# The last pair's second layer directly behind its first, and w_out by product in DRAM, in a decayed linear attention with a softplus feed-forward layer

## The chip, the cores and the metric

One core of one Trainium2 chip runs the whole program. The metric is device time in microseconds (us). The kernel before took 552.56 us in the median of three runs (551.27, 552.56 and 556.31).

## What is computed

The reference, cut to what matters: a linear attention with per-head decay over blocks of 64 positions, 4 sequences of 768 positions with 8 heads of 64, and on its output x (3072 tokens by 512) two layers with a softplus between them.

```python
for b in range(nb):                                   # 12 blocks of 64
    intra = einsum('bhic,bhjc->bhij', qb, kb) * Dmask
    intra = einsum('bhij,bhjd->bhid', intra, vb)
    inter = einsum('bhid,bhde->bhie', qb * lam_pow, kv_state)
    out[:, :, sl] = intra + inter
    kv_state = lam_block * kv_state + einsum('bhsd,bhse->bhde', kb * rev_pow, vb)
h = x @ w_in                                          # 3072x512 @ 512x2048
g = maximum(h, 0) + log1p(exp(-abs(h)))
y = g @ w_out                                         # 3072x2048 @ 2048x512
```

## The kernel before, in words

The program makes x in six chunks of 512 columns (c = 0 to 5), each from four head pairs; a unit g is one chunk of one head pair. Each chunk goes through the two layers in three pairs of chunks, (0,1), (2,3) and (4,5), which the code names 0, 2 and 4. Every float32 operand of the layers is split into a rounded part and a rest (`hi` on ScalarE, `lo` on VectorE), and each product is three TensorE matmuls (`m`, `n`: three per quarter in chunk pair 0; `product` and `out_product`: three per piece).

For pairs 2 and 4 the first layer, and for all pairs the second, multiplies blocks of two by two with seven products instead of eight, P1 to P7, as Strassen's method does in the form with few sums. The sums of weight blocks that it needs are made on VectorE (`in_sums`, `second_sums`), split, and kept in DRAM: `g1`, `g2` for w_in, `v_sums` (four sums per block i) and `g3` (the plain w_out, by block i) for w_out. `load_w1` reads back both parts for a block i of the first layer. `load_v(c, p, m)` reads what product p of the second layer needs for four blocks, one half m: for P5, P6, P7 and P3 one DMA of 1 MB from `v_sums`, for P1, P2 and P4 four DMAs of 256 KB from `g3`.

The softplus outputs of a pair are eight tiles `act` of 1 MB, one per block i, each with four quarters. Pairs 0 and 2 write them to DRAM (`put_by`, steps `wr` and `wrm`) and read them back by quarter (`fetch`, step `rd`, into tiles `back`); pair 4's stay in SBUF until used.

On-chip tiles come from fixed places. The tables `homes` give each new tile its place (21 of 8 KB per partition, `b8`, and smaller kinds), so a tile that takes a place waits for the last reader of the tile before it, also where that reader is a DMA that stores it.

The order of all work but the last two second layers is a written list of some 1500 steps, each a word and its numbers, which one loop turns into instructions; an engine runs its own in that order. Words that matter here: `L` loads weights or a unit; `xy`, `z`, `x`, `y` are attention on TensorE; `pr`/`px` are the first layer's products of pairs 2 and 4 and `cu2`, `cu3`, `c1` the ScalarE copies of a product out of PSUM, `u2b`, `c11` and so on VectorE sums; `s11` to `s22` softplus, `t3` a VectorE difference; `sumB`, `plB`, `sndB` make, split and send block i of `v_sums`; `w1`, `w1c` are `load_w1`; `lvb`, `thb`, `tlb`, `ob` are load, `hi`, `lo` and products of the second layer in the list. In the kernel before that is pair 0, from tiles `back`, mixed with the end of pair 4's first layer. Behind the list a loop does the second layers of pairs 4 and 2, one product after another; at the start of each it loads the weights of the next, and `fetch_at` says when pair 2's outputs are read back. The last matmuls are cut into two halves of 256 columns, so that the sum and the store of the first half overlap the second half.

All loads and nearly all stores are issued by one queue, SP's, in the list's order.

Of the kernel before, what the change touches and what calls it, by code (L numbers as in the profile page):

```python
# [32 lines left out]
def decay_attention_softplus_ffn(  # L33
# [236 lines left out]
    def w_hi(*ks):  # L270
        nc.scalar.copy(out=w_at(ks)[:, 0], in_=c_at(ks).bitcast(F32))

    def w_lo(*ks):
        w = w_at(ks)
        nc.vector.tensor_sub(out=w[:, 1], in0=c_at(ks).bitcast(F32), in1=w[:, 0])

    def w_of(f, which):
        j, i = divmod(w_order.index((f, which)), 2)
# [531 lines left out]
    for c, word in ((0, "b"), (2, ""), (4, "c")):  # L810
# [11 lines left out]
        "thb": lambda p, i: split_hi(0, p, i), "tlb": lambda p, i: split_lo(0, p, i),
        "thc": lambda i: split_hi(4, "P1", i), "tlc": lambda i: split_lo(4, "P1", i), "lvc": lambda m: load_v(4, "P1", m),
        "lvb": lambda p, m: load_v(0, p, m),
        "ob": lambda p, i: [out_product(0, p, i, n) for n in range(2)],
        "tkb": lambda p, n: taking(0, p, n),
        "sdb": lambda p, n: send(*taken[0, p, n], n, nc.sync),
# [6 lines left out]
    for line in """  # L834
        scan 3, scan 1, scan 0, scan 2, mk64, Lq 3, x 3, a 3, Lq 0, lpm, L A0, scale A0, shift A0, lps, x 0, Lv 3, z 3,
        xh 3, Lq 1, a 0, xl 3, round A0, Lk 0, Lv 0, Lk 3, x 1, k 0, sign A0, add A0, Lq 2, L A2, a 1, L A3, Lv 2,
        L u4, Lk 1, Lk 2, Lv 1, k 3, z 0, xh 0, rp1, y 0, xl 0, lamc, y 3, st 0, x 2, hi A0, lo A0, st 3, scale A2 A3,
        m 0 0, a 2, z 2, round A2 A3, shift A2 A3, sign A2 A3, xh 2, xl 2, add A2 A3, m 0 2, k 4, xy 4, q 4, L A1, a 4,
        k 1, m 0 3, k 2, uh 4, hi A2 A3, lo A2 A3, y 1, st 1, z 4, xh 4, xl 4, round A1, y 2, scale A1, m 2 3, m 2 0,
        shift A1, ul 4, m 2 2, st 2, L u5, k 5, m 3 0, z 1, xh 1, xy 5, q 5, sign A1, add A1, hi A1, L u8, k 8, q 8,  # L840
        n 0 0, xl 1, m 0 1, m 2 1, uh 5, a 5, ul 5, L u7, q 7, lo A1, z 5, L A4, xy 8, act 0, xh 5, act 2, xl 5, a 8,
        m 1 2, m 3 1, uh 8, ul 8, L A5, kv 8, scale A4 A5, m 3 3, shift A4 A5, n 2 0, k 7, sign A4 A5, m 1 3,
        round A4 A5, add A4 A5, z 8, xr 8, L B0, xy 7, hi A4 A5, m 1 1, uh 7, a 7, ul 7, m 1 0, act 1, n 2 1, lo A4 A5,
        sum 1, n 0 1, n 1 0, L u6, k 6, q 6, m 3 2, act 3, z 7, xh 7, xl 7, xy 6, uh 6, L B1, L u9, m 4 0, sum 2,
        m 4 2, m 4 1, kv 9, n 0 3, a 6, L A8, scale B0 B1, m 4 3, q 9, L A9, act 4, n 2 3, ul 6, z 6, k 9, xh 6, xl 6,
        ph 1, pl 1, L u10, xy 9, L A7, m 5 0, a 9, kv 10, L u12, k 10, L A6, n 2 2, bct 2, uh 9, m 5 3, ul 9, n 1 2,
        scale A8 A9, shift A8 A9, sign A8 A9, scale A6 A7, n 1 1, shift A6 A7, n 0 2, n 1 3, bct 1, n 3 3, z 9, bct 0,
        L A11, xy 10, a 10, sA 0, n 5 3, L u11, sign A6 A7, xr 9, round A6 A7, add A6 A7, k 11, round B0 B1,
        round A8 A9, L u13, uh 10, ul 10, L A10, ph 2, n 4 3, n 5 2, scale A10 A11, n 3 2, n 5 0, q 10, add A8 A9,
        pl 2, n 4 2, n 5 1, shift B0 B1, n 4 0, bct 5, n 4 1, L A13, hi A6 A7, L A12, z 10, t3b 0, bct 4, sA 1, xr 10,  # L850
        xy 11, m 5 2, kv 11, kv 12, n 3 0, n 3 1, bct 3, lo A6 A7, snd 1, L A14, n 7 3, n 6 0, m 5 1, k 12, n 6 3,
        shift A10 A11, q 11, snd 2, uh 11, ul 11, sign A10 A11, round A12 A13, a 11, act 5, round A10 A11, add A10 A11,
        n 6 2, n 7 0, xy 12, z 11, hi A10 A11, m 6 3, a 12, uh 12, ul 12, m 6 2, sum 5, m 7 2, L A15, m 7 3,
# [186 lines left out]
```

## Time and profile before

| what | value |
|---|---|
| median of three runs | 552.56 us |
| profiled execution, its own time | 560.41 us |
| its span, first to last instruction | 558.6 us |
| TensorE busy | 540.0 us, 97% of the span |
| VectorE, ScalarE busy | 423.4 us, 311.5 us |
| moved by DMA | 180.08 MB, mean 322 GB/s |
| mean granted TensorE clock | 0.997 |

The profile is of one execution, and that one took 7.85 us more than the median of the runs. "Idle before" in a row is the time that an engine stood still just before the group's instructions, with what ended it. Matmuls overlap in the record: one of 512 columns lasts some 390 ns from start to end, but the next starts sooner, so the pace is busy time by count. A TensorE clock of 1.00 is 2.4 GHz, 0.50 is 1.2 GHz.

### The profile page before, as it was taken

The numbers are of one execution on the slowest core, as the hardware profiler recorded it, in microseconds if no ns is written. First come the engines' busy times: TensorE is split into PE (matmuls) and PEld (weight loads), VectorE is DVE, ScalarE is ACT, GpSimd is POOL, SyncE is SP. The second block draws the span as 40 slices with busy tenths as digits, with TensorE's granted clock in tenths as the row PEclk, the third lists the DMA queues.
The fourth block names the chain that finished last, engine by engine and source line by source line (L and its number), as shares of the span: only waits on it lengthen the run. The fifth ranks groups of instructions, "written<-read, shape, count | busy, mean of one in ns | idle before, by whom it ended". The sixth has DMA issues, their size and how long they took to land.

```text
span 558.6 us, 11757 instructions
## 1 busy us (share of the span) xinstructions
PE 540.0 (97%) x4777; PEld 441.9 (79%) x4777; DVE 423.4 (76%) x681; ACT 311.5 (56%) x520; POOL 0.4 (0%) x5
## 2 busy tenths in 40 slices
PE   8989998999999997999998999998999999999997
PEld 6668887888888886888886778887878888888886
DVE  6898899899966768797743588686795796865982
ACT  4855875666755467677533636654554445455440
POOL 0000000000000000000000000000000000000000
PEclk9999999999999999999998999999999999999999
DMA  8998999999999999999999999968298799983751
GB/s 304 402 407 341 322 346 381 350 408 373 337 394 381 375 380 364 402 325 397 378 368 336 283 345 371 366 217 266 86 318 311 237 385 342 374 318 94 246 191 74
DMA packets 76424, 180.08 MB, mean 322 GB/s; under 512 B 5074, under 2 KB 25810, under 8 KB 71762
## 3 DMA queue, kind: packets, MB, share of 16 engines
q1 hardware_dynamic: 75648, 178.15, 88.1%
q10 hardware_dynamic: 722, 1.18, 0.6%
q8 instruction: 38, 0.62, 0.4%
q14 instruction: 16, 0.13, 0.1%
HBM read 124.78 MB, written 54.53 MB: 321 GB/s over the span
## 4 chain that ended last, share of the span: by engine, by line
PE 74%; DMA 16%; DVE 4%; ACT 2%; issue 2%; SPq 1%; ACTq 0%; DVEq 0%
PE h L460 16%; PE r2P L709 14%; PE r4P L709 12%; PE r0P L709 11%; PE x L585 9%; PE c L585 4%; DMA att<-in_att 3%; DMA v_sums<-box 3%; PE x L364 2%; DMA v0P<-v_sums 2%; DMA g<-w 2%; PE a L585 2%; DMA back<-kept 2%; PE z L378 2%; PE z L382 2%
## 5 line engine op out<-in xcount | busy, mean ns | idle before, releaser
L460 PE MATMUL h<-x,w 128*128 128x512 f32 x384 | 93.5, 397 | 2.5 <-issue 1.4
L460 PEld LDWEIGHTS h<-x,w 128*128 128x128 f32 x384 | 70.6, 188 | 19.4 <-issue 2.3
L709 PE MATMUL r0P<-s0P,v0P 128*128 128x512 f32 x336 | 77.5, 390 | 2.7 <-DMA v0P<-v_sums 2.5
L709 PE MATMUL r2P<-s2P,v2P 128*128 128x512 f32 (+1 forms) x348 | 76.7, 382 | 0.5 <-DVE post L991 0.5
L709 PE MATMUL r4P<-s4P,v4P 128*128 128x512 f32 x336 | 76.6, 390 | 0.3 <-DMA v4P<-v_sums 0.3
L709 PEld LDWEIGHTS r0P<-s0P,v0P 128*128 128x128 f32 x336 | 62.8, 188 | 16.9 <-ACT s0P L675 3.2
L709 PEld LDWEIGHTS r2P<-s2P,v2P 128*128 128x128 f32 x348 | 63.9, 188 | 13.4 <-DVE post L991 0.7
L709 PEld LDWEIGHTS r4P<-s4P,v4P 128*128 128x128 f32 x336 | 63.0, 188 | 13.7 <-ACT s4P L675 0.7
L675 ACT CAST s0P<-back 128x512 fp32r<-128x512 f32 x40 | 24.0, 620 | 31.5 <-PE r0P L709 11.3
L675 ACT CAST s2P<-back 128x512 fp32r<-128x512 f32 x40 | 24.3, 622 | 23.8 <-PE r2P L709 9.8
L675 ACT CAST s4P<-act 128x512 fp32r<-128x512 f32 x40 | 24.7, 622 | 21.8 <-PE r4P L709 10.2
L680 DVE TENSOR_TENSOR s4P<-act,s4P 128x512 fp32r<-128x512 f32 x40 | 26.8, 688 | 13.0 <-ACT s4P L675 12.9
L680 DVE TENSOR_TENSOR s2P<-back,s2P 128x512 fp32r<-128x512 f32 x40 | 26.5, 687 | 12.1 <-ACT s2P L675 12.1
L777 ACT COPY ta<-x 128x512 f32<-128x512 f32 x32 | 18.4, 586 | 30.1 <-PE x L585 30.1
L763 ACT ACTIVATE act<-act 128x512 f32<-128x512 f32 x48 | 29.7, 631 | 6.6 <-DVE act L766 5.7
L395 DVE SCALAR_TENSOR_TENSOR st<-st,lam_c,y 64x256 f32<-64x256 f32 x72 | 31.7, 479 | 2.1 <-PE x L364 1.0
L680 DVE TENSOR_TENSOR s0P<-back,s0P 128x512 fp32r<-128x512 f32 x40 | 26.3, 686 | 8.9 <-ACT s0P L675 8.5
L763 ACT ACTIVATE act<-h 128x512 f32<-128x512 f32 x32 | 18.9, 597 | 25.1 <-PE h L460 25.1
L585 PE MATMUL x<-xc4P,w1a 128*128 128x512 f32 x96 | 25.4, 406 | 2.4 <-ACT ta L777 2.4
L766 DVE TENSOR_TENSOR act<-c,ta 128x512 f32<-128x512 f32 x16 | 10.9, 686 | 18.3 <-PE c L585 18.3
L364 PE MATMUL x<-att 64*64 64x64 f32 x640 | 24.7, 221 | 0.0
L364 PEld LDWEIGHTS x<-att 64*64 64x64 f32 x640 | 21.8, 135 | 3.2 <-issue 3.2
(144 smaller groups left out, 951.3 us busy)
## 6 DMA issues: line engine op xcount, KB each, us to landing
att<-in_att SPq DMA_DIRECT2D x44, 512.0 KB, 7.9
raw<-in_wts SPq DMA_DIRECT2D x32, 512.0 KB, 8.4
kept<-act SPq DMA_DIRECT2D x16, 1024.0 KB, 7.7
back<-kept SPq DMA_DIRECT2D x16, 1024.0 KB, 9.7
g<-w SPq DMA_DIRECT2D x24, 512.0 KB, 9.5
w1a<-g SPq DMA_DIRECT2D x12, 1024.0 KB, 8.6
w1b<-g SPq DMA_DIRECT2D x12, 768.0 KB, 7.8
g<-box SPq DMA_DIRECT2D x16, 512.0 KB, 8.6
```

What stands on the lines that cost most here:

```text
L364: nc.tensor.matmul(x[r, cols], lhsT=k[r, b, t], rhs=q[r, b, t], start=True, stop=True)
L378: nc.tensor.matmul(w[half(t), s, cols], lhsT=st[r, b, t], rhs=qd[r, b, t], start=True, stop=False)
L382: nc.tensor.matmul(w[half(t), s, cols], lhsT=v[r, b, t], rhs=a[r, b, t], start=False, stop=True,)
L395: nc.vector.scalar_tensor_tensor(out=to[:, :, t], in0=of[:, :, t], scalar=lam_c[r, h : h + 1], in1=u[:, :, t], op0=ALU.mult, op1=ALU.add,)
L460: nc.tensor.matmul(to, lhsT=w[:, i, cs], rhs=x[:, j, :], start=not done and n == 0, stop=len(done) == NP - 1 and n == 2,)
L585: nc.tensor.matmul(to, lhsT=first_weights(c, name, i, k, p), rhs=x[:, j, p], start=start and p == 0 and m == 0, stop=p == 1 and m == 2, sk ...
L675: nc.scalar.copy(out=g[:, 0], in_=of)
L680: nc.vector.tensor_sub(out=g[:, 1], in0=of, in1=g[:, 0])
L709: nc.tensor.matmul(to[:, cols], lhsT=w[:, k, x, n * 128 : n * 128 + 128], rhs=g[:, y, cols], start=fresh and m == 0, stop=count == NF // 2 ...
L763: nc.scalar.activation(to, of, AF.Softplus)
L766: nc.vector.tensor_add(out=act_of(c, i)[1], in0=firsts[c, "c", i], in1=p1u2[c, i][:, 1])
L777: nc.scalar.copy(out=p1u2[c, i][:, n] if n < 2 else act_of(c, i)[3], in_=firsts[c, "x", i])
```

## The change

Three things. The second layer in the list becomes pair 4's, and its products' inputs are the tiles `act` that the first layer has just made; pair 0's moves into the loop behind the list, ahead of pair 2's, so its fetches do too. The plain w_out lies in DRAM by product (`v_even` for P1, `v_odd` for P2 and P4), so each half is one DMA of 1 MB, and the odd half of the even blocks, which no product reads, isn't stored; the layout of the split tiles follows. And the list and the tables `homes` are new throughout. Of these tables and the list only single lines are shown.

```diff
         "bh": [
-            0, 1, 2, 3, 4, 0, 2, 3, 1, 4, 0, 1, 3, 2, 4, 0, 1, 3, 2, 4,
+            0, 1, 2, 3, 4, 1, 3, 2, 0, 4, 1, 0, 2, 3, 4, 1, 0, 2, 3, 4,
...
-        return w_pairs[j][:, :, i : i + len(ks)]
+        if w_order[ks[0]][1]:
+            w = w_pairs[j].rearrange("q n s (m c) -> q n s m c", m=2)[:, i : i + len(ks)]
+            return [w[:, :, :, m] for m in range(2)]
+        return [w_pairs[j][:, m, i : i + len(ks)] for m in range(2)]
...
-    g3 = [dr.tile([128, 2, 2, DM], F32, name=f"g3_{i}", tag=f"g3_{i}") for i in range(NF // 2)]
+    v_even = dr.tile([128, NF // 2, 2, 256], F32, name="v_even", tag="v_even")
+    v_odd = dr.tile([128, 2, NF // 2, 2, 256], F32, name="v_odd", tag="v_odd")
...
     def store_second(i):
-        for n in range(2):
-            nc.sync.dma_start(out=g3[i][:, n], in_=w_of(2 * i + n, 1).bitcast(F32))
+        w = w_pairs[w_order.index((2 * i, 1)) // 2].bitcast(F32).rearrange("q n s (m c) -> q n s m c", m=2)
+        nc.sync.dma_start(out=v_even[:, i], in_=w[:, 0, 0])
+        nc.sync.dma_start(out=v_odd[:, :, i], in_=w[:, 1])
...
-            odd, side = {"P1": (0, 0), "P2": (1, 0), "P4": (1, 1)}[p]
-            for k in range(4):
-                nc.sync.dma_start(
-                    out=t[:, k].bitcast(F32), in_=g3[4 * m + k][:, odd, :, side * 256 : side * 256 + 256]
-                )
+            of = {"P1": v_even, "P2": v_odd[:, 0], "P4": v_odd[:, 1]}[p]
+            nc.sync.dma_start(out=t.bitcast(F32), in_=of[:, 4 * m : 4 * m + 4])
...
-        "t2b": lambda i: second_t2(0, i), "tsb": lambda p, i: split_sum(0, p, i),
+        "t2b": lambda i: second_t2(4, i), "tsb": lambda p, i: split_sum(4, p, i),
...
-        px P3 2, u2bc 2, w1c 0, px P1 0, px P5 0, thb P1 6, thb P1 7, s22c 6, px P2 1, phB 5, c1c 0, px P6 0, lvb P1 1,
+        px P1 1, sB 5, cu2c 2, c1c 1, sumB 7, phB 7, c11c 2, px P7 2, cu3c 2, s12c 6, s22c 3, s11c 2, plB 7, sndB 7,
...
-    todo = [(c_, p, i) for c_ in (4, 2) for p in order for i in range(NF // 2)]
+    todo = [(c_, p, i) for c_ in (0, 2) for p in order for i in range(NF // 2)]
...
-    runs = [(c_, p) for c_ in (4, 2) for p in order]
-    fetch_at = {4: 0, 5: 1, 7: 2, 9: 3}
+    runs = [(c_, p) for c_ in (0, 2) for p in order]
+    fetch_at = {0: (0, 2), 2: (0, 3), 4: (2, 0), 5: (2, 1), 7: (2, 2), 9: (2, 3)}
```

How the instructions stand. Names carry a number at their end that only tells tiles apart; `w1a5` is the first part of block 5 of the first layer's weights, `att23` the last unit of the attention, `kept1<-act2_2` the store of pair 2's block 2, `box1_3` the sums of w_out's block 3. The first place is SP's queue where the first layer of pair 2 asks for its last blocks of weights. Before:

```order
L549 DMA v_sums_122<-box1_1_2666 128x2048
L123 DMA att23_2994<-in_att 128x1024 x2
L559 DMA w1a4_3004<-g1_4_102 128x2048
L560 DMA w1b4_3005<-g2_4_110 128x1536
L647 DMA kept1_124<-act2_2_2751 128x2048
L559 DMA w1a5_3042<-g1_5_103 128x2048
L560 DMA w1b5_3043<-g2_5_111 128x1536
```

Now:

```order
L123 DMA att23_2874<-in_att 128x1024 x2
L568 DMA w1a4_2893<-g1_4_102 128x2048
L569 DMA w1b4_2894<-g2_4_110 128x1536
L568 DMA w1a5_2988<-g1_5_103 128x2048
L569 DMA w1b5_2989<-g2_5_111 128x1536
L656 DMA kept1_118<-act2_0_2517 128x2048
L656 DMA kept1_118<-act2_2_2759 128x2048
L163 DMA raw14_3077<-in_wts 128x1024
L558 DMA v_sums_116<-box1_3_3015 128x2048
```

The store of act2_2 no longer stands between the two blocks of weights; block 5 follows block 4 directly, and the place that it takes is free sooner. On ScalarE, at the same stretch of the changed kernel (xc4P6 takes the place in SBUF that box1_3 had; x2_5 is the PSUM bank of block 5, copied out into act2_5). Before:

```order
L763 ACTIVATE act2_5_3158<-act2_5_3158 128x512
L777 COPY ta44_3326<-x4_4_3313 128x512
L629 CAST xc4P6_3341<-tt4_0_3201 128x512
L629 CAST xc4P6_3341<-tt4_1_3221 128x512
L763 ACTIVATE act2_4_3175<-x2_4_3021 128x512
```

Now:

```order
L638 CAST xc4P5_3218<-tt4_0_3073 128x512
L638 CAST xc4P6_3221<-tt4_0_3073 128x512
L783 COPY act2_4_3216<-x2_4_3002 128x512
L769 ACTIVATE act2_4_3216<-act2_4_3216 128x512
L783 COPY act2_5_3207<-x2_5_3131 128x512
```

The cast of xc4P6 moved ahead of the last copies of pair 2's blocks 4 and 5. The second place is ScalarE at the end of pair 4's first layer, where the second layer's splits begin (x4_1, x4_2 are banks of pair 4, ta41 and ta42 the copies that free them, s0P1 and s4P1 the split input of the second layer's product P1). Before:

```order
L763 ACTIVATE act4_3_3605<-x4_3_3468 128x512
L777 COPY ta42_3651<-x4_2_3644 128x512
L675 CAST s0P1_4_3682<-back00_1_3680 128x512
L777 COPY act4_2_3708<-x4_2_3644 128x512
L777 COPY ta41_3737<-x4_1_3721 128x512
L763 ACTIVATE act4_2_3708<-act4_2_3708 128x512
```

Now:

```order
L274 CAST w12_3678<-c12_3488 128x4x256
L684 CAST s4P1_3_3680<-act4_3_3584 128x512
L684 CAST s4P1_4_3682<-act4_4_3385 128x512
L783 COPY ta42_3685<-x4_2_3648 128x512 x2
L783 COPY ta41_3707<-x4_1_3697 128x512
L549 CAST box1_7_3709<-box1_7_3709 128x4x256
```

The splits stand at the same place, but read tiles that ScalarE itself wrote some rows earlier instead of a tile that a DMA fills. The third place is SP's queue where the last sums of w_out go to DRAM and come back. Before:

```order
L651 DMA back00_0_3805<-kept0_123 128x4x512
L549 DMA v_sums_122<-box1_5_3710 128x2048
L651 DMA back01_0_3873<-kept0_123 128x4x512
L693 DMA v0P1_0_3875<-g3_0_114 128x2x256
L693 DMA v0P1_0_3875<-g3_1_115 128x2x256
L693 DMA v0P1_0_3875<-g3_2_116 128x2x256
L693 DMA v0P1_0_3875<-g3_3_117 128x2x256
L651 DMA back01_1_3917<-kept0_123 128x4x512
L549 DMA v_sums_122<-box1_6_3861 128x2048
L689 DMA v0P6_0_3952<-v_sums_122 128x4x512
L689 DMA v0P6_1_3960<-v_sums_122 128x4x512
```

Now:

```order
L701 DMA v4P2_1_3860<-v_odd_115 128x2048
L558 DMA v_sums_116<-box1_5_3813 128x2048
L701 DMA v4P2_0_3896<-v_odd_115 128x2048
L698 DMA v4P5_0_3978<-v_sums_116 128x4x512
L660 DMA back01_1_3997<-kept0_117 128x4x512
L558 DMA v_sums_116<-box1_6_3821 128x2048
L698 DMA v4P6_1_4060<-v_sums_116 128x4x512
```

Four DMAs per half of P1's weights became one, three of the four fetches left this stretch, and from the matmul that releases the last store of sums to the first that needs what it wrote TensorE's order now has 126 matmuls of 512 columns, 72 before.

## Rows read from the trace of the kernel before

**Rows 1.** Page, part 1: busy time of the engines.
```profile
span 558.6 us, 11757 instructions
...
PE 540.0 (97%) x4777; PEld 441.9 (79%) x4777; DVE 423.4 (76%) x681; ACT 311.5 (56%) x520; POOL 0.4 (0%) x5
```

**Rows 2.** Waits of TensorE: engine, line <- releaser: us in total, times, longest.
```profile
PE x L585 <- DMA w1a<-g: 2.9, 1, 2.9
PE r0P L709 <- DMA v0P<-v_sums: 2.5, 2, 1.5
PE x L585 <- ACT ta L777: 2.4, 1, 2.4
PE z L382 <- issue: 1.7, 2, 1.0
...
PE h L460 <- issue: 1.4, 1, 1.4
...
PE r4P L709 <- DMA v4P<-v_sums: 0.3, 1, 0.3
```

**Rows 3.** Stretches: busy time (instructions) by engine, then PEclk, DMA share, GB/s.
```profile
188.25:190.27 2.02, 2.02 (x113) 1.96 (x112) 1.59 (x4) 1.91 (x4) 0.00 (x0) 1.00 0.91 333
336.00:350.00 14.00, 14.00 (x64) 11.54 (x63) 11.21 (x19) 8.73 (x16) 0.00 (x0) 1.00 1.05 374
...
298.00:301.00 3.00, 0.59 (x4) 0.17 (x2) 0.58 (x1) 1.72 (x4) 0.00 (x0) 0.99 1.01 426
301.00:304.00 3.00, 3.00 (x7) 2.40 (x8) 0.11 (x1) 2.89 (x5) 0.00 (x0) 0.50 0.83 313
```

**Rows 4.** The chain that ended last: start us, us, what.
```profile
148.15 2.72 PE x L585 x12
...
214.79 8.58 DMA w1a<-g
...
288.27 10.94 DMA back<-kept
...
300.92 4.60 PE x L585 x12
...
322.15 7.08 DMA v_sums<-box
329.28 6.17 DMA v0P<-v_sums
```

**Rows 5.** Timeline of ScalarE (start us, us, [idle before]).
```profile
299.28 0.62 ACT L675 CAST s0P<-back 128x512 fp32r<-128x512 f32 x1 [8.30 <-DMA back<-kept]
...
300.28 0.59 ACT L777 COPY ta<-x 128x512 f32<-128x512 f32 x1
```

**Rows 6.** Groups of instructions, shapes apart: xcount | busy us, mean ns | idle before.
```profile
L709 PE MATMUL r2P<-s2P,v2P 128*128 128x512 f32 x324 | 73.6, 389 | 0.0
...
L395 DVE SCALAR_TENSOR_TENSOR st<-st,lam_c,y 64x256 f32<-64x256 f32 x72 | 31.7, 479 | 2.1 <-PE x L364 1.0
...
L544 DVE TENSOR_TENSOR box<-box 128x1024 fp32r<-128x1024 f32 x14 | 17.1, 1218 | 0.9 <-ACT box L540 0.9
L658 DVE TENSOR_TENSOR act<-act 128x512 f32<-128x512 f32 x24 | 16.3, 686 | 2.2 <-ACT act L763 2.2
...
L777 ACT COPY ta<-x 128x512 f32<-128x512 f32 x32 | 18.4, 586 | 30.1 <-PE x L585 30.1
```

**Rows 7.** DMA issues, median us to landing (page, part 6).
```profile
kept<-act SPq DMA_DIRECT2D x16, 1024.0 KB, 7.7
...
w1a<-g SPq DMA_DIRECT2D x12, 1024.0 KB, 8.6
```

**Rows 8.** By tile: v_sums from 195 to 262 us, its DMAs.
```profile
L549 SPq DMA_DIRECT2D v_sums<-box x3: 333/382/1117, 199.7 to 235.2; - x3
...
DMA to landing us min/median/max: 5.2/7.9/10.0
```

**Rows 9.** By tile: kept from 150 to 420 us, stores and loads together.
```profile
DMA to landing us min/median/max: 6.0/7.8/13.1
```

More of the change, by code (lines that the diff above doesn't have):

```diff
@@ L270, in w_hi, with c_like_w, w_of @@
     def w_hi(*ks):
-        nc.scalar.copy(out=w_at(ks)[:, 0], in_=c_at(ks).bitcast(F32))
+        nc.scalar.copy(out=w_at(ks)[0], in_=c_like_w(ks))
     def w_lo(*ks):
[L274 to L278, printed above, removed]
+        hi, lo = w_at(ks)
+        nc.vector.tensor_sub(out=lo, in0=c_like_w(ks), in1=hi)
+    def c_like_w(ks):
+        c = c_at(ks).bitcast(F32)
+        return c.rearrange("q n (s c) -> q n s c", s=2) if w_order[ks[0]][1] else c
+    def w_of(f):
+        j, i = divmod(w_order.index((f, 0)), 2)
         return w_pairs[j][:, :, i]
@@ L820, in decay_attention_softplus_ffn @@
     steps_of |= {
-        "t2b": lambda i: second_t2(0, i), "tsb": lambda p, i: split_sum(0, p, i),
[L822 to L827, printed above, removed]
+        "t2b": lambda i: second_t2(4, i), "tsb": lambda p, i: split_sum(4, p, i),
+        "thb": lambda p, i: split_hi(4, p, i), "tlb": lambda p, i: split_lo(4, p, i),
+        "thc": lambda i: split_hi(0, "P1", i), "tlc": lambda i: split_lo(0, "P1", i), "lvc": lambda m: load_v(0, "P1", m),
+        "lvb": lambda p, m: load_v(4, p, m),
+        "ob": lambda p, i: [out_product(4, p, i, n) for n in range(2)],
+        "tkb": lambda p, n: taking(4, p, n),
+        "sdb": lambda p, n: send(*taken[4, p, n], n, nc.sync),
     }
@@ L840, in decay_attention_softplus_ffn @@
[L840 to L844, printed above, removed]
@@ L850, in decay_attention_softplus_ffn @@
[L850 to L853, printed above, removed]
-        scale A14 A15, ph 5, n 6 1, sA 3, lo A10 A11, xr 11, q 12, bct 6, L u15, n 7 2, sign B0 B1, sA 2, hi A8 A9,
@@ new lines, in decay_attention_softplus_ffn @@
+        st 3, y 0, z 2, xh 2, sign A2 A3, add A2 A3, lamc, st 0, k 4, xl 2, x 1, m 0 2, xy 4, a 1, Lk 1, m 0 0,
+        hi A2 A3, lo A2 A3, q 4, m 2 2, L A1, k 2, m 2 0, k 1, m 3 2, scale A1, a 4, Lv 1, uh 4, z 4, xh 4, ul 4,
+        shift A1, xl 4, y 1, sign A1, st 1, round A1, y 2, st 2, m 3 0, L u5, k 5, L u8, q 8, q 5, m 3 3, z 1, xh 1,
+        xl 1, L A5, k 8, L A4, xy 5, a 5, kv 8, m 2 3, n 2 0, m 2 1, act 2, uh 5, ul 5, add A1, hi A1, lo A1, L u7,
+        z 5, xh 5, xy 8, scale A4 A5, m 0 1, xl 5, q 7, round A4 A5, m 3 1, n 2 1, shift A4 A5, L u10, n 1 0, uh 8,
@@ new lines, in decay_attention_softplus_ffn @@
+        a 8, ul 8, act 3, L A6, m 1 2, m 1 0, sign A4 A5, add A4 A5, k 7, z 8, xy 7, L A9, act 0, uh 7, L u6, L A7,
+        m 1 1, hi A4 A5, lo A4 A5, m 1 3, act 1, n 0 1, a 7, ul 7, n 0 0, k 6, m 4 0, m 4 3, xy 6, xr 8, L B0, L u9,
+        sum 2, z 7, xh 7, a 6, xl 7, m 4 2, m 4 1, L A10, k 9, L A11, uh 6, kv 9, n 2 3, n 0 3, k 10, q 6, act 4, z 6,
+        xh 6, L B1, ul 6, xl 6, xy 9, uh 9, L A14, round A6 A7, scale A6 A7, n 5 0, n 0 2, L A15, bct 0, ph 2, n 5 3,
+        a 9, L u11, round A10 A11, n 1 3, shift A6 A7, sign A6 A7, scale A10 A11, round A14 A15, n 2 2, scale B0 B1,
@@ new lines, in decay_attention_softplus_ffn @@
+        n 1 1, ul 9, m 5 2, n 1 2, bct 1, L A8, xy 10, q 9, z 9, scale A14 A15, shift A10 A11, m 5 3, add A6 A7, n 3 1,
+        uh 10, ul 10, n 5 1, q 10, L u12, sign A10 A11, sA 1, L u13, add A10 A11, sA 0, n 3 3, k 11, bct 2, q 11,
+        n 4 0, hi A6 A7, a 10, xr 9, scale A8 A9, shift A8 A9, n 5 2, t3b 0, kv 10, n 4 3, hi A10 A11, lo A10 A11,
+        n 4 1, xy 11, z 10, m 5 0, a 11, kv 11, n 3 2, sA 2, n 3 0, bct 5, k 12, shift B0 B1, lo A6 A7, xr 10, m 5 1,
+        bct 3, L A13, sum 1, n 4 2, round A8 A9, m 6 3, bct 4, uh 11, ul 11, t3b 2, L A12, m 6 2, round A12 A13,
@@ new lines, in decay_attention_softplus_ffn @@
+        shift A14 A15, m 6 1, scale A12 A13, act 5, q 12, n 6 2, wr 0, round B0 B1, z 11, xr 11, xy 12, n 7 1, m 6 0,
+        act 6, ph 1, pl 2, kv 13, a 12, uh 12, ul 12, n 7 0, L u14, m 7 0, n 6 1, sign B0 B1, add B0 B1, sA 5, n 7 3,
+        sign A8 A9, m 7 3, sA 3, kv 12, m 7 1, m 7 2, k 13, add A8 A9, xy 13, t3b 1, sum 5, z 12, act 7, L u15, xr 12,
+        hi A8 A9, lo A8 A9, n 7 2, k 14, bct 7, n 10 3, n 10 2, wr 2, kv 14, n 6 3, n 6 0, m 9 0, hi B0 B1, n 10 1,
+        shift A12 A13, snd 2, m 9 1, m 10 3, a 13, bct 6, q 13, uh 13, ul 13, n 10 0, n 11 0, wr 1, n 11 1, m 10 2,
@@ new lines, in decay_attention_softplus_ffn @@
+        m 8 1, n 13 3, n 9 3, k 16, n 9 2, n 14 2, n 9 0, xbh P1 1, xy 16, q 16, d1 1, bct 9, t3b 4, z 15, wr 5,
+        xbh P1 0, m 8 0, xr 15, d2 1, d4 1, xbl P1 0, m 8 2, kv 16, m 12 3, L B3, m 12 0, act 8, xbl P1 1, uh 16,
+        bct 13, q 17, a 16, ul 16, snd 0, snd 3, round B2 B3, n 12 0, xbh P3 0, n 12 1, snd 1, n 15 1, sA 6, m 12 1,
+        xbh P2 1, n 12 2, xbl P2 1, L B4, wr 4, L u18, xbh P2 0, xbl P2 0, scale B2 B3, m 12 2, shift B2 B3, xbl P3 0,
+        d2 0, n 12 3, sum 7, bct 12, n 14 3, n 14 0, n 14 1, bct 14, k 17, n 15 0, pl 4, xbh P4 1, d4 0, d3 1,
@@ new lines, in decay_attention_softplus_ffn @@
+        xbh P3 1, xbh P6 1, n 15 2, m 14 1, n 15 3, act 12, m 13 2, L B5, m 13 0, sign B2 B3, m 13 3, xy 17, ph 7,
+        xbl P3 1, pl 7, xbl P4 1, a 17, xbh P4 0, snd 4, z 16, xbh P6 0, L u19, m 13 1, uh 17, act 13, xbl P6 0, kv 17,
+        pr P1 7, c1 7, add B2 B3, L B8, xbl P6 1, t3b 6, xbh P7 1, xbl P7 1, L B9, xbh P5 0, xbl P5 0, bct 15, ul 17,
+        kv 18, t3b 7, sum 6, m 14 0, m 15 1, m 15 0, m 15 2, xr 16, m 14 2, sumB 0, scale B4 B5, m 15 3, k 18, pr P6 7,
+        z 17, sA 7, xy 18, wr 6, xbh P7 0, m 14 3, xbh P5 1, xbl P5 1, act 14, q 18, pr P2 7, c11 7, pr P5 7, snd 7,
@@ new lines, in decay_attention_softplus_ffn @@
+        act 15, cu2 7, xbl P7 0, pr P7 7, pr P1 6, k 19, uh 18, ul 18, ph 6, kv 19, xr 17, a 18, xbl P4 0, cu3 7,
+        pr P4 7, c1 6, wr 7, pl 6, pr P6 6, shift B4 B5, z 18, xy 19, a 19, cu2 6, pr P7 6, pr P5 6, scale B8 B9,
+        s21 7, w1 0, phB 0, w1 1, pr P2 6, u3b 7, pr P3 7, c11 6, cu3 6, plB 0, pr P4 6, s21 6, u2b 7, snd 6, L u20,
+        pr P1 0, u3b 6, q 19, pr P5 0, s22 6, shift B8 B9, c1 0, pr P2 0, c11 0, pr P6 0, cu2 0, xr 18, sndB 0,
+        pr P1 1, c1 1, pr P7 0, s11 7, cu3 0, pr P3 6, uh 19, pr P4 0, L u21, sign B4 B5, sign B8 B9, u3b 0, u2b 6,
@@ new lines, in decay_attention_softplus_ffn @@
+        z 23, xr 23, ybh P3 1, ybh P1 0, pr P6 5, sumB 1, pr P7 4, cu2 5, t3 3, pr P7 5, phB 1, ybl P3 0, g4 0, wrm 1,
+        c11 5, pr P5 4, c11 4, ybh P5 0, plB 1, ybh P6 0, pr P5 5, ybl P5 0, ybl P1 0, cu3 4, s11 4, u3b 4, cu3 5,
+        e1 1, pr P4 5, g3 0, L B12, u3b 5, pr P4 4, ybh P2 1, ybl P2 1, sndB 1, s21 5, g3 1, ybh P5 1, g2 1, g4 1,
+        ybh P2 0, wrm 3, ybl P2 0, ybl P6 0, pr P3 4, u2b 4, s22 4, px P1 4, ybh P7 0, pr P3 5, ybh P4 0, s21 4,
+        ybl P7 0, ybh P6 1, ybl P6 1, scale B12 B13, c1c 4, ybh P7 1, s12 4, ybl P4 0, L B11, hi B8 B9, px P1 5, c1c 5,
@@ L972, in decay_attention_softplus_ffn @@
             if j in fetch_at:
-                fetch(2, fetch_at[j], m)
+                fetch(*fetch_at[j], m)
         while late:
```

152 lines of the change are left out of this document (61 added, 91 removed), and 44 rows, old and new, of the table homes.

## The prediction, made before the changed kernel was run

> **What bounds the kernel now.** First the busy times [rows 1]: TensorE works 540.0 of 558.6 us, VectorE and ScalarE far less. So the time is TensorE's, and the change can only take from what TensorE loses: 18.6 us in which it stands still, and stretches in which it runs below its pace. The pace is in the groups [rows 6]: 324 matmuls of 512 columns in 73.6 us, 0.227 us each, and a stretch of the second layer in the middle of the program, 336 to 350 us, has TensorE busy for 14.00 of 14.00 us at clock 1.00 [rows 3]. No order of steps makes that shorter. Both kernels have the same matmuls: the change alters what lies between them.
>
> Next, who TensorE waited for [rows 2]. Three waits are on DMA or on an engine held by one: 2.9 us for first-layer weights, 2.5 us in two pieces for second-layer sums, 2.4 us for a ScalarE copy. Issue, a wait for nothing that the profile shows, has 1.7 and 1.4; 0.3 is at the start of pair 4's product P6. The rest of the 18.6 is the start, where inputs land, and the tail behind the last matmul; the change does little there, so I put it at nothing.
>
> Then the chain [rows 4], which gives each wait its cause. The weights of block 5 were asked for at 214.79 and landed 8.58 us later, at 223.37. The copy: ScalarE stood 8.30 us before a cast of a fetched tile [rows 5], because that tile's load took 10.94 us [rows 4], and the copy of PSUM that TensorE needed was queued behind the cast. The sums: a store of 7.08 us, and right behind it the load of 6.17 us of what it wrote.
>
> The second of these has an echo. From 301 to 304 us the granted clock is 0.50, that is 1.2 GHz [rows 3], right behind the stretch 298 to 301 in which TensorE was busy for 0.59 of 3.00 us; twelve matmuls that take 2.72 us elsewhere take 4.60 there [rows 4]. That is 1.9 us more.
>
> **The change part by part.** *What goes.* The weights of block 5 follow block 4 in SP's queue, with no store between, and the order has more work in front of their use: from the last TensorE instruction that their place waits for to their first matmul there were 24 matmuls of 512 columns and one attention step; now there are 42 and two. 42 x 0.227 = 9.5 us, an attention step is 2.02 us [rows 3], so 13.5 us. Three ScalarE passes of about 0.6 [rows 6] lie ahead of the load, some 1.8, which leaves 11.7 us for a landing of 8.6 [rows 7]. The 2.9 us go.
>
> The cast that held ScalarE reads a tile of pair 4 that ScalarE itself has just written, and no fetch stands in front of the copies any more: the 2.4 us go, and the slow clock behind them, 1.9.
>
> The sums: 72 matmuls, 16.3 us, stood between the release of the last store and the use of what it wrote; the two transfers took 7.08 + 6.17 = 13.3 us, the split ahead of them 1.2 [rows 6], and the load also queued behind others. Now it is 126, 28.6 us. The second piece was the weights of P5's second half, with 48 matmuls, 10.9 us; now 144. The 2.5 us go.
>
> Sum of what goes: 2.9 + 2.4 + 1.9 + 2.5 = 9.7 us.
>
> *What is only moved.* Pair 4's softplus, its differences `t3` and the splits are the same instructions. VectorE is 11.21 of 14 us busy in the stretch of 336 to 350 [rows 3], so it has room, but the first products of the second layer now depend on outputs made just before. Between the last piece of a block of pair 4 and the use of that block in P1 the order keeps several other products (for block 0 some fourteen, 19 us), against four passes of 0.6 to 0.7 us. I put this at nothing; if that cover failed, one chain of four passes would be exposed, 2.6 us. The loop behind the list gets two more fetches per early product; the weights of its first one, P6, have 48 matmuls before their use in both kernels, and waited 0.3 us [rows 2]. I leave that 0.3.
>
> *w_out by product.* 72 loads of 256 KB become 18 of 1 MB, so SP issues 54 DMAs fewer, and 2 MB less are written. No wait above is left that this would shorten; the hi and lo passes write the same 1024 elements per partition in another order, as the split of the sums already does at 1218 ns [rows 6]. Bounds: 0, and the 3.1 us of issue waits if those came from the crowded queue. I take 0.
>
> *What the change adds.* Buffers are now reused right behind a store in two places of pair 2's first layer, which the trace of before doesn't have. First, block 1's outputs take the place of block 6's: 42 matmuls and an attention step, 11.5 us, from the release of the store to the matmul that needs the copy; on the way four VectorE passes and two short ones or a copy, about 3.6 us, so 7.9 are left for a store that takes 7.7 [rows 7]. Nothing, just. Second, and tighter: the cast of xc4P6 takes the place of box1_3, whose store waits for a mask and a split, 0.7 + 1.2; then cast, copy, softplus, copy on ScalarE, 2.4 us, must pass before TensorE may write the bank of block 5 again. Queued behind the cast are just those copies, and TensorE waits for the last. There are 42 matmuls and about half an attention step, 10.5 us; 10.5 - 1.9 - 2.4 = 6.2 us are left for the store. In that stretch three such stores took 5.2, 7.9 and 10.0 us [rows 8]: the wait is 0 to 3.8, with the middle one 1.7. I take 1.7.
>
> [...]
>
> **The sum.** In the profiled execution: 560.41 - 9.7 + 1.7 = 552.4 us. The runs are shorter than that execution, 552.56 in the median, 7.85 less. TensorE's losses in it were 18.6 us standing and 1.9 in the slow clock, 20.5; if the 7.85 came out of these, 12.65 remain, 0.62 of them. I scale both terms so: 552.56 - 0.62 x 9.7 + 0.62 x 1.7 = 552.56 - 6.0 + 1.1 = 547.6 us, 0.9% less. About 1% is what a measurement of this kernel can tell from no change; faster by more than that begins at 547.0.
>
> **The rivals.** *All of it comes off.* The waits that go are structural (a load asked for too late), so they may be as long in the runs as in the profile, and the new place may not wait: 552.56 - 9.7 = 542.9. For it: the lead of block 5's weights before was only some 7.5 us (24 x 0.227 + 2.02) against 8.6. Against: the runs don't have room for all of it beside the start, the tail and the issue waits.
>
> *It is given back.* The waits were three of many near misses; a new order has others in their place, with the same loads in the same time: 549 to 556, say 552. For it: a DMA share around 1.0 [rows 3], so landings stay late wherever they are. Against: in the new order no load between the start and the loop has less than 10.9 us of TensorE's work in front of it; before, several had 5 to 9.5.
>
> *Slower: the stores hold the buffers.* At the two places above, every us by which a store lands later than 7.9 and 6.2 us is a us of TensorE. At 13.1, the longest in its view [rows 9], and 10.0 [rows 8] the price is 5.2 + 3.8 = 9.0, and 1.9 of slow clock behind each, 12.8: 3.1 more than the 9.7 saved, 552.56 + 3.1 = 555.7 us. It decides from new waits of 9.7 us on. For it: ScalarE and SP serve in order, so one late store holds all behind it. Against: the median store leaves 0 and 1.7.
>
> Whether such a wait costs its length or more hangs on the clock. In the trace the wait of 2.4 us had the clock fall to 0.50 behind it [rows 3]. The Trainium skill, "TensorE: Matmul & The Clock Gate", section "HAM oscillation — how this bites in real kernels", has idle gaps of TensorE bring the lower clock for the work behind them; the trace agrees at that wait. [...]
>
> **How the numbers follow.** The forecast, part of the waits gone and little added (545 to 550), has 0.54; of that I put 0.22 below 547.0. All of it off: 0.18, all faster. Given back: 0.16, of which 0.13 within 1% and 0.03 slower. The stores: 0.12, 0.07 within 1% and 0.05 slower. Together faster by over 1% 0.40, within 1% 0.52, slower 0.08. The range from 543 to 553 takes in the first case's end, the given-back case's middle and both bounds of the new wait; above it lies most of the slower case.
>
> **What would show it.** In the changed kernel's list of waits the row for w1a, the row of ScalarE's copy and that of the sums should be gone or below 0.5 us each, and no stretch behind 300 us should have a clock below 0.9. The turn from first to second layer should read 14.00 of 14.00. If a new wait shows, I expect it on a ScalarE copy while pair 2's block 5 is multiplied, near 230 us, with a store of v_sums ahead of it. I am wrong if TensorE's idle total stays near 18 us, or if VectorE becomes what TensorE waits for in pair 4's second layer.

## The result and the profile after

The changed kernel takes 550.66 us in the median of 20 runs (549.34 to 553.45). The kernel before, in 20 runs beside it, takes 556.75 (551.27 to 561.30); the three runs shown above are among these, and two of them lie low. The ratio is 0.991, with a 95% interval of 0.989 to 0.993: 0.9% less, within 1%, and near the forecast of 0.9%. The spread has shrunk with the median: 10 us between the fastest and the slowest run before, 4 now. The profiled execution's own time is 551.27 us.

Busy times of the changed kernel (page, part 1), against [rows 1]:

```profile
span 549.5 us, 11637 instructions
...
PE 538.4 (98%) x4777; PEld 441.8 (80%) x4777; DVE 423.2 (77%) x681; ACT 311.7 (57%) x520; POOL 0.4 (0%) x5
```

TensorE stood still for 18.6 us before (16.3 in a second profile of the kernel before, below) and does for 11.1 now. Its busy time fell by 1.6: the slow clock of [rows 3] is gone, and a new stretch of slow clock near 55 us (below) takes part of that back. Who it waits for (engine, line, releaser: us in total, times, longest), against [rows 2]:

```profile
PE h L467 <- issue: 2.1, 1, 2.1
PE warm_ps L181 <- DVE warm L176: 1.5, 1, 1.5
PE z L389 <- issue: 1.0, 1, 1.0
```

The three rows on w1a, on the copy ta and on v_sums are gone, and no row is left that names a DMA. What remains is the start, the tail and issue. The stretches of [rows 3] now (busy by engine, then PEclk, DMA share, GB/s):

```profile
336.00:350.00 14.00, 14.00 (x64) 11.58 (x63) 10.56 (x17) 6.55 (x11) 0.00 (x0) 1.00 0.97 355
298.00:301.00 3.00, 3.00 (x15) 2.46 (x14) 2.19 (x5) 3.00 (x7) 0.00 (x0) 1.00 0.72 265
301.00:304.00 3.00, 3.00 (x15) 2.49 (x14) 2.93 (x6) 2.02 (x4) 0.00 (x0) 1.00 0.92 236
```

The turn from the first layer to the second is full, as predicted. One transfer shows by how much: the last store of sums, alone in this view of v_sums from 316 to 317 us,

```profile
L558 SPq DMA_DIRECT2D v_sums<-box x1: 2317/2317/2317, 316.2 to 316.2; - x1
...
DMA to landing us min/median/max: 14.1/14.1/14.1
```

took 14.1 us, 7 more than the same store in [rows 4], and TensorE did not wait.

### The profile page after: what moved, and what is told of

Same layout as the page of the kernel before. It is cut to its first block, busy times and chain, and to the rows that moved or that the text cites. A ratio compares the mean times of both kernels' runs of the same rounds, so it can differ in the third digit from the quotient of the medians.

```text
span 549.5 us, 11637 instructions
## 1 busy us (share of the span) xinstructions
PE 538.4 (98%) x4777; PEld 441.8 (80%) x4777; DVE 423.2 (77%) x681; ACT 311.7 (57%) x520; POOL 0.4 (0%) x5
## 4 chain that ended last, share of the span: by engine, by line
PE 93%; DVE 5%; issue 1%; ACT 0%; DVEq 0%
PE h L467 16%; PE x L594 15%; PE r2P L715 14%; PE r0P L715 14%; PE r4P L715 14%; PE c L594 8%; PE a L594 4%; PE x L371 3%; PE z L385 2%; PE z L389 2%; PE y L373 1%; DVE xc2P L641 1%; PE z L360 1%; DVE st L402 1%; DVE masks L208 0%
## 5 line engine op out<-in xcount | busy, mean ns | idle before, releaser
L715 PE MATMUL r0P<-s0P,v0P 128*128 128x512 f32 x336 | 76.4, 389 | 0.0
L594 PE MATMUL x<-xc4P,w1a 128*128 128x512 f32 x96 | 23.9, 389 | 0.0
L594 PE MATMUL x<-xc4P,w1b 128*128 128x512 f32 x96 | 23.6, 389 | 0.0
```

The costliest lines, as they stand in the source:

```text
L594: nc.tensor.matmul(to, lhsT=first_weights(c, name, i, k, p), rhs=x[:, j, p], start=start and p == 0 and m == 0, stop=p == 1 and m == 2, sk ...
L715: nc.tensor.matmul(to[:, cols], lhsT=w[:, k, x, n * 128 : n * 128 + 128], rhs=g[:, y, cols], start=fresh and m == 0, stop=count == NF // 2 ...
```

## The experiments

Every ratio below is to the kernel before, in runs beside it.

**Is it the layout?** One run has the kernel before with w_out by product, one the changed kernel with w_out by block: the hunks on `g3`, `v_even`, `v_odd`, `store_second`, `load_v` and the views of the split tiles, put in or taken back as they stand in the diff above.

> The kernel before with w_out by product in DRAM and nothing else: the old list, the old tables. Theory (the gain is the three late landings that the new order no longer waits for; the layout is worth nothing): ratio to before 0.997 to 1.003, and TensorE's waits on w1a, on the copy ta and on v_sums stay, 5 to 8 us together. Rival (54 DMAs fewer and some 19,000 fewer small packets make every landing earlier, and that is the gain): ratio 0.989 to 0.994 and these waits under 2 us together.

> The changed kernel with the plain w_out by block again, as before: four loads of 256 KB per half, 2 MB more stored. Theory: ratio to before 0.988 to 0.994, as the changed kernel, and no wait of TensorE on a DMA or on a copy above 0.5 us behind 60 us. Rival (layout): ratio 0.996 to 1.00 and such waits of 3 us or more.

Measured: 0.999 (0.995 to 1.003) and 0.989 (0.985 to 0.992). TensorE's waits with the old order and the new layout:

```profile
PE x L594 <- ACT w L274: 2.4, 1, 2.4
PE r0P L715 <- DMA v0P<-v_even: 1.7, 1, 1.7
...
PE x L594 <- DMA w1a<-g: 1.0, 1, 1.0
PE r0P L715 <- DMA v0P<-v_sums: 1.0, 1, 1.0
```

The waits stay, 6.1 us of them, though not all as expected: one is on a load of the new form, and the longest, at 223 us where w1a was waited for before, is on a ScalarE split. The new order with the old layout has no wait on a DMA behind 60 us. The layout is worth nothing beyond the intervals in either direction; the gain is the order's.

**Do the three causes, taken away one by one, make the gain?** In the kernel before, steps were moved and every tile kept its place. First all three:

```diff
-c1 4, wrm 2, kv 23, w1 5, k 23
+c1 4, kv 23, w1 5, wrm 2, k 23
-cu2c 2, rd 0 1, thb P1 4, sndB 7 ... c1c 1, px P6 1, s11c 2, px P4 2
+cu2c 2, rd 0 1, sndB 7 ... c1c 1, px P6 1, s11c 2, thb P1 4, px P4 2
-ob P1 4, thb P1 0, tlb P1 0, sumB 6 ... tlb P1 2, rd 1 0 ... ob P1 1, phB 6, plB 6 ... ob P1 5, sndB 6
+ob P1 4, sumB 6, phB 6, plB 6, thb P1 0, tlb P1 0 ... tlb P1 2, sndB 6, rd 1 0 ... ob P1 1 ... ob P1 5
```

> The kernel before, with pair 0 still in the list and the old layout, but the three causes taken away by moving six steps: the store of act2_2 behind the load of w1 5, the cast of the fetched tile behind two copies, and the last sums of w_out made, split and sent ahead of the splits of fetched tiles. Theory: the three waits and the slow clock behind the second one go, 9.7 us of the profile or some 6 of the runs: ratio 0.987 to 0.993, as the changed kernel, and the three rows gone from TensorE's waits or under 0.5 us each. Rival (given back: in the old order the next late landing takes the place of each, and only the reordering of the pairs and the whole new list makes room): ratio 0.996 to 1.00, with new rows of 2 us or more on DMA or on ScalarE.

Measured: 1.016 (1.012 to 1.021), 9.7 us slower in the median. Its waits:

```profile
PE r0P L709 <- DMA v0P<-g: 7.3, 1, 7.3
PE c L585 <- DVE act L769: 2.9, 1, 2.9
PE x L585 <- DMA w1a<-g: 2.0, 3, 1.3
```

The 7.3 us are a wait for a load of P1's weights. It was issued just behind VectorE's last pass over the sums, for which SP's queue had stood 10.3 us (VectorE's timeline, SP's waits from 310 to 330 us, the chain):

```profile
317.32 1.23 DVE L544 TENSOR_TENSOR box<-box 128x1024 fp32r<-128x1024 f32 x1 [2.29 <-ACT box L540]
```

```profile
SPq L549 <- DVE box L544: 10.3, 1, 10.3
```

```profile
319.48 8.87 DMA v0P<-g
```

The store of the sums, moved forward in SP's queue, stood in front of P1's loads and held them until that pass was done. So each move was then run alone; of the third, the store stayed where it was and only its VectorE and ScalarE steps moved.

> The kernel before with one step moved: the cast of the fetched tile (thb P1 4) behind the copies cu3c 2, c1c 1 and s11c 2 instead of ahead of them. Theory (that cast held ScalarE, and with it the copy that TensorE waited for): the wait on ta and the slow clock behind it go, 4.3 us of the profile, 2.5 to 4.3 of the runs: ratio 0.992 to 0.996. Rival (given back: TensorE runs into the next late landing that much sooner): 0.998 to 1.002, with a longer wait on v0P in place of the one on ta.

> The kernel before with the last sums of w_out made and split ahead of the splits of fetched tiles (three steps moved on VectorE and ScalarE), their store left where it was in SP's queue. The store then starts some 4 to 5 us sooner. Theory: the wait of 1.5 us on v_sums goes, perhaps the second one of 1.0 too, 1 to 2.5 us of the runs: ratio 0.995 to 0.998. Rival (given back): 0.999 to 1.003.

> The kernel before with the store of act2_2 behind the load of block 5's weights in SP's queue, as in the changed kernel, and nothing else. In the run with all three moved, three waits on w1a of 2.0 us together were left near here, and a wait of 2.9 us came on a tile whose place that store holds. Theory as corrected by that run (a late landing goes only where the order has room for it; a move alone hands the lateness on): ratio 0.998 to 1.008, the wait on w1a under 1.5 us and a wait of 1 to 3 us behind the store. Rival (my first reading, the store ahead was the cause and its removal is the gain): 0.993 to 0.997.

Measured: 1.001 (0.998 to 1.005), 1.001 (0.998 to 1.003) and 1.008 (1.005 to 1.011). No cause taken away alone gives anything beyond the intervals in the old order. In the profile with the sums sooner the waits on v_sums were 1.1 us in place of some 2.5, but 1.2 on a ScalarE split and on a load of the plain w_out had come. What the third move runs into is in the chain that ended last of its profile (start us, us, what):

```profile
217.59 10.59 DMA kept<-act
228.19 0.33 SPq L163
...
228.58 6.23 DMA v_sums<-box
234.83 0.62 ACT xc4P L629
...
238.26 5.86 PE c L585 x18
```

The store of act2_2, now later, holds what follows it; the store of box1_3 holds the cast of xc4P6, which takes its place, and the copies behind that cast keep TensorE 3.5 us. This need not be all of the 4 us by which these runs are slower: the same profile lost 2.0 us on an attention input near 18 us with a slow clock behind, where the order is that of before, and 2.0 on the copy ta. It is the mechanism of the rival "the stores hold the buffers", at a place that I had thought only the new order had.

**Was the copy ta a fair sample?** The kernel before once more, for its profile.

> The kernel before once more, for its profile. In the profile that the prediction read, the wait on the copy ta and the slow clock behind it were 4.3 us; no other profile of the old order has had it, while waits of 1 to 3 us on w1a and on v_sums came in each. If that wait was one late landing of one execution, it is absent here and the execution is nearer to 556 us; if it belongs to the order, it is there with 2 us or more.

Measured: 555.08 us. Its waits, and the cast of the fetched tile on ScalarE (start us, us, [idle before]):

```profile
PE r0P L709 <- DMA v0P<-v_sums: 2.6, 2, 1.4
PE x L585 <- DMA w1a<-g: 2.6, 1, 2.6
```

```profile
296.07 0.62 ACT L675 CAST s0P<-back 128x512 fp32r<-128x512 f32 x1 [5.61 <-DMA back<-kept]
```

The waits on w1a and v_sums are there in full, the one on ta isn't. The cast stood 8.30 us in the first profile [rows 5], where TensorE waited 2.4, and 5.61 here, where it waited for nothing: some 6 us are covered. The expectation was wrong on the other profiles of the old order. That of before_w1_first has this wait too, 2.0 us, because the cast stood longer:

```profile
301.78 0.62 ACT L675 CAST s0P<-back 128x512 fp32r<-128x512 f32 x1 [7.87 <-DMA back<-kept]
```

So it is a near miss of the old order, which some executions hit and others not. And the wait on w1a is not in each of them: in before_cast_later, whose order is that of before up to some 290 us, TensorE waited at this place for ScalarE alone, in an execution of 552.42 us:

```profile
PE x L585 <- ACT act L763: 1.0, 1, 1.0
```

With before_by_product, six profiles have the old order there, and each lost between 1.0 and 3.5 us around this place.

**Where the difference lies.** Stretches of before_again, then of the changed kernel (busy by engine, PE first; the last three are PEclk, DMA share, GB/s):

```profile
20.00:60.00 40.00, 37.19 (x839) 30.13 (x840) 33.30 (x57) 24.99 (x47) 0.00 (x0) 1.00 0.94 363
60.00:180.00 120.00, 118.51 (x1700) 97.88 (x1699) 105.89 (x167) 80.09 (x128) 0.00 (x0) 1.00 0.99 367
180.00:240.00 60.00, 57.43 (x721) 47.44 (x720) 45.16 (x71) 38.37 (x66) 0.00 (x0) 1.00 0.99 382
300.00:390.00 90.00, 87.29 (x383) 71.33 (x382) 64.89 (x104) 48.20 (x84) 0.00 (x0) 1.00 0.89 302
```

```profile
20.00:60.00 40.00, 36.63 (x838) 29.35 (x836) 30.45 (x52) 23.10 (x47) 0.00 (x0) 0.96 0.92 359
60.00:180.00 120.00, 119.57 (x1722) 98.57 (x1716) 108.64 (x174) 78.58 (x125) 0.00 (x0) 1.00 1.00 362
180.00:240.00 60.00, 59.66 (x729) 48.84 (x728) 44.25 (x71) 41.77 (x74) 0.00 (x0) 1.00 0.97 362
300.00:390.00 90.00, 90.00 (x399) 74.53 (x398) 68.98 (x112) 49.26 (x85) 0.00 (x0) 1.00 0.80 284
```

TensorE's idle time falls by 2.2 us from 180 to 240, by 2.7 from 300 to 390 and by 1.1 from 60 to 180; it grows by 0.6 from 20 to 60, where 1.25 of slow clock come on top (below). With 0.4 more at the start, before 20 us, that makes 2.2 + 2.7 + 1.1 - 0.6 - 1.25 - 0.4 = 3.75, and the two executions differ by 555.08 - 551.27 = 3.81. The 1.1 was a wait on issue near 94 us, so most of what was gained is the 2.2 and the 2.7. The medians lie 6.1 apart; where the other 2.3 us go is not shown by these two profiles. From 300 to 390 the DMA share falls as well, 0.89 to 0.80: four fetches are left there of seven. By tile, back from 300 to 390 us, before_again and then the changed kernel:

```profile
L651 SPq DMA_DIRECT2D back<-kept x7: 359/413/2674, 302.1 to 350.4; - x7
```

```profile
L660 SPq DMA_DIRECT2D back<-kept x4: 360/370/2730, 314.3 to 371.4; - x4
```

So there are two candidates for that stretch, the traffic and the lead (TensorE's work between a transfer's start and its use).

**Traffic or lead?** One run puts traffic back into the new order, one takes it out of the old, one shortens a lead in the new.

```diff
...
+    def more(k):
+        nc.sync.dma_start(out=extra[k], in_=kept[0][:, 4 * (k % 2) : 4 * (k % 2) + 4, k // 2])
...
-lvb P1 1, px P7 1 ... lvb P2 1, tlb P5 3 ... rd 1 1, tlb P5 0 ... lvb P6 1, thb P2 4
+lvb P1 1, more 0, px P7 1 ... lvb P2 1, more 1, tlb P5 3 ... rd 1 1, more 2, tlb P5 0 ... lvb P6 1, more 3, thb P2 4
```

> The changed kernel with four loads of 1 MB more, from kept0 into DRAM that nobody reads, on SP's queue between 300 and 335 us, where the kernel before had its fetches. Nothing waits for them. Theory A (traffic: the fetches that left this full stretch for the loop are what made the landings there early enough): TensorE waits again on v4P or on splits behind it, 2 to 5 us, ratio to before 0.994 to 0.999. Theory B (lead: 126 and 144 matmuls in front of the loads carry landings that are some 5 us later): no wait above 0.5 us in 285 to 390 us, ratio 0.988 to 0.992.

```diff
-        nc.sync.dma_start(out=back[c, n, m], in_=kept[c // 2][:, 4 * m : 4 * m + 4, n])
+        k = 4 if c else 1
+        nc.sync.dma_start(out=back[c, n, m][:, 0:k], in_=kept[c // 2][:, 4 * m : 4 * m + k, n])
+        if c == 0:
+            nc.gpsimd.memset(back[c, n, m][:, 1:4], 1.0)
```

> The kernel before with the eight fetches of pair 0's outputs cut to a quarter each (one block of four, 256 KB instead of 1 MB; GpSimd fills the rest, so that the later steps have something to read): 6 MB less between 288 and 362 us, the same order and the same leads. What it computes for pair 0 in three of four blocks is left out. Theory A: the losses of TensorE between 300 and 390 us, 3 to 5 us in the profiles of the kernels with the old order, fall under 1 us: ratio 0.992 to 0.996. Theory B: the waits on v_sums stay, 1 us or more each, ratio 0.997 to 1.001.

```diff
-ob P1 3, plB 6, thb P1 0 ... tlb P5 1, sndB 6, t2b 6
+ob P1 3, thb P1 0 ... tlb P5 1, plB 6, sndB 6, t2b 6
```

> The changed kernel with one VectorE step moved: the lower part of the last sums of w_out (plB 6) directly ahead of its store, some 15 us later, so that about 11 us are left from the store to the first product that needs what it wrote, instead of 26. Theory (lead in TensorE's work against the two transfers): store and load took 7.1 + 6.2 before and 14.1 + 7.6 in the changed kernel, so the wait on v4P6 comes back with 2 to 10 us, with a slow clock behind it: 1 to 8 us of the runs, ratio to before 0.993 to 1.004. Rival (that stretch is served quickly now since three fetches left it, the lead is not what counts): no such wait, ratio 0.989 to 0.992.

Measured: 0.994 (0.992 to 0.997) with more traffic, 0.997 (0.994 to 0.999) with light fetches, 0.994 (0.991 to 0.997) with the late sums. The stretch 300 to 390 with more traffic, and the wait that came:

```profile
PE r4P L720 <- DMA v4P<-v_sums: 2.4, 2, 1.5
```

```profile
300.00:390.00 90.00, 87.63 (x386) 71.92 (x385) 67.54 (x110) 46.95 (x80) 0.00 (x0) 1.00 0.86 320
```

Four copies that nobody waits for bring back a loss of 2.4 us: with them the leads of 126 and 144 matmuls are no longer enough. They act in two ways, which this run does not part. The loads of v4P from v_sums took 14.7 us to landing in the median of the stretch from 300 to 375, and 9.9 in the changed kernel; and one copy held SP's queue itself, so that the last store of the sums was issued at 321.14 us instead of 316.21 (SP's timeline):

```profile
313.88 7.15 SPq L665 DMA_DIRECT2D extra<-kept  x1
```

The old order with light fetches, the other way round:

```profile
PE r0P L712 <- DMA v0P<-v_sums: 1.4, 1, 1.4
```

```profile
300.00:390.00 90.00, 88.20 (x388) 72.37 (x387) 64.71 (x104) 48.89 (x85) 9.64 (x7) 1.00 0.72 237
```

At a DMA share of 0.72, lower than the changed kernel's, one of the two waits on v_sums is left and 1.8 us stay lost. The runs gain 2.5 us (556.38 to 553.93): fewer bytes help the old leads, but are not all of it. And with the lead cut from some 26 us to 11 in the new order, TensorE waits 1.8 us on v4P, though the store landed in 4.0 us there, and the clock is 0.66 in the 3 us behind:

```profile
PE r4P L715 <- DMA v4P<-v_sums: 1.8, 1, 1.8
```

```profile
348.00:351.00 3.00, 3.00 (x10) 2.35 (x9) 0.81 (x2) 0.62 (x1) 0.00 (x0) 0.66 1.05 401
```

This profiled execution, 558.03 us, was the longest of its runs, by a wait of 3.8 us on issue near 60 us; the ratio is from all of them. Neither theory holds alone. Each half, taken away, costs the changed kernel some 2 us (0.994 twice against 0.991); the intervals overlap at their ends.

**And the weights of block 5?** The changed kernel with their load behind the two stores:

```diff
-xr 21, w1 5, t3 0 ... phB 3, wrm 2, L B13
+xr 21, t3 0 ... phB 3, wrm 2, w1 5, L B13
```

> The changed kernel with the load of block 5's weights behind the two stores of act2_0 and act2_2 in SP's queue, as it stood behind one store before. In the changed kernel it was issued at 212.4 us, landed 4.8 us later and was needed at 224.2; the second of the two stores was issued at 221.2. Theory (that TensorE no longer waits there comes from the place in SP's queue): it is issued near 221.7 and lands 4.8 to 9 us later, so TensorE waits 2 to 6 us on w1a, with up to 2 us of slow clock behind, and nothing later gives it back: ratio to before 0.993 to 1.002. Rival (the places and the rest of the order do it, and SP's order there does not matter): 0.988 to 0.992, no wait on w1a above 0.5 us.

Measured: 1.006 (1.004 to 1.009), 558.96 us, 8.3 more than the changed kernel. The wait, and the two groups of matmuls behind it in the chain:

```profile
PE a L594 <- DMA w1a<-g: 5.7, 1, 5.7
```

```profile
228.60 2.93 PE a L594 x6
231.53 2.56 PE x L594 x6
```

```profile
228.00:231.00 3.00, 2.40 (x6) 1.92 (x7) 0.00 (x0) 0.00 (x0) 0.00 (x0) 0.50 0.99 320
```

Twelve matmuls in 5.49 us, 2.72 at full clock [rows 4], are 2.8 lost behind the wait of 5.7, together 8.5: as much as the whole loss. Nothing later gave it back: the span is 7.0 us longer, though TensorE had come to this place 1.4 us sooner than in the changed kernel. SP's order at this one place decides over the 2.2 us of the stretch 180 to 240, and behind two stores it costs more than it did before behind one.

**The loss near 52 us.** The changed kernel has a new one there (TensorE's timeline; the instruction queue in the 1 us from 51 on; the clock behind):

```profile
54.40 3.29 PE L467 MATMUL h<-x,w 128*128 128x512 f32 x9 [2.12 <-issue]
```

```profile
q8 instruction: 1, 0.02, 6.7%
```

```profile
55.00:58.00 3.00, 3.00 (x22) 1.98 (x23) 0.29 (x1) 0.60 (x1) 0.00 (x0) 0.59 0.80 289
```

A wait with no releaser, a transfer of the queue named instruction just ahead, and nine matmuls in 3.29 us that take 9 x 0.227 = 2.04 at full clock. I thought the spacing of the attention steps was the cause:

```diff
-act 4, z 6 ... round A10 A11, n 1 3, shift A6 A7 ... scale B0 B1, n 1 1, ul 9
+act 4, n 1 1, n 1 3, z 6 ... round A10 A11, shift A6 A7 ... scale B0 B1, ul 9
```

> The changed kernel with two quarters of the first layer (n 1 1, n 1 3, six matmuls) moved from behind to ahead of the attention of unit 6, so that 18 matmuls of 512 columns stand between two attention steps near 51 us, as before and as elsewhere, instead of 12. There the profiles show TensorE still for 2.1 to 3.6 us with no releaser, right behind a transfer of the queue named instruction, and a slow clock behind it. Theory (attention's many short instructions run TensorE's code out while its fetch is late): the wait shrinks to under 1.5 us and the clock there stays above 0.9: 1 to 3 us less than the changed kernel, ratio to before 0.984 to 0.988. Rival (the place is a chance of that fetch and not of the spacing): ratio 0.988 to 0.992, the wait there or at a neighbour.

Measured: 0.992 (0.989 to 0.995), 551.63 us, and the wait is longer:

```profile
PE h L467 <- issue: 3.2, 1, 3.2
```

The spacing is not it. Nor is the transfer by itself: the profile of before has one in the 1 us from 50 on, and TensorE does not wait there. What sets this wait stays open.

No version here beats the changed kernel beyond the intervals.

## Why the prediction was right, and where it was not

**The time.** 4.96 us less than the runs shown was forecast, and 6.1 less than the median of the runs beside it was measured. The forecast of 547.6 missed 550.66 by 3.1 because three low runs were taken for the level of before. As a ratio it was right, 0.991, but in part by luck: the copy ta and the added wait were counted too high, the scaling took off 0.38 of each term, and the start was put at nothing; these errors offset each other.

**What goes.** The waits on w1a and on v_sums were rightly read, cause and size: 2.9 and 2.5 us in the first profile, 2.6 and 2.6 in the second, none in the changed kernel. In before_cast_later the first was 1.0 us on ScalarE, so it too varies between executions. The part of the load's place in SP's queue is shown by after_w1_late. For the sums I named the lead of 126 and 144 matmuls; after_sums_late has the wait back without it, and after_more_traffic shows that it was only half: the change also took fetches out of the full stretch, which I had counted at nothing.

**The copy ta and its slow clock, 4.3 us**, was the wrong term. I took a wait of one execution for one of the kernel; the next profile of it had none. The cause, a cast behind a late fetch, was read rightly, but it costs only what the landing is late beyond some 6 us. Scaling all terms by 0.62 hid this. The profiled execution lay 7.85 us above the median shown, but only 3.7 above the one of 20 runs (560.41 - 556.75), and 5.3 above before_again (560.41 - 555.08); this term of 4.3 is most of either. Taken out, with the other two unscaled, 2.9 + 2.5 = 5.4 us would have been left, beside the measured 6.1. That the spread narrowed because such near misses are gone is likely, but not shown.

**The added wait, 1.7 us at xc4P6**, did not come. The stores of v_sums there landed like this (by tile, 195 to 262 us), against [rows 8]:

```profile
L558 SPq DMA_DIRECT2D v_sums<-box x2: 319/319/319, 227.1 to 233.9; - x2
...
DMA to landing us min/median/max: 4.0/4.8/5.7
```

I had 6.2 us for it and took 7.9 from the old order's rows. These stores landed in 5.7 at most, and the one at 316 us took 14.1, though the DMA share was much the same (0.88 from 226 to 234 us, 0.84 from 314 to 332). The median of three stores in the old order was no forecast for the new one.

**What was put at nothing.** w_out by product: right, by two runs. Pair 4's softplus and splits: right, no row of TensorE's waits names them. The traffic in the full stretch: wrong, as said. The start: wrong by some 2 us, 0.6 more idle from 20 to 60 and 1.25 of slow clock.

**The rivals.** "All of it off" is what the waits show, but not the time: 4.3 of its 9.7 us were there in some executions only, and the start took 2 us back. "Given back" is what the single moves in the old order did, 1.001 twice: there other waits come in their place; that its leads are too short everywhere is argued and not shown. "The stores hold the buffers" is real, but it was the old order that had it, in before_w1_first. "TensorE's idle total near 18" did not come: 11.1, against 18.6 and 16.3 in the two profiles of before.
